# Linear recurrence and soft mixture of experts on one core: the last three groups of tokens regrouped, and the engines' written orders drawn up anew

## The chip, the core and the metric

The kernel runs on one core of a Trainium2 chip. A core has a matrix engine (TensorE), a vector engine (VectorE), an engine for activation functions (ScalarE), an engine for general work (GpSimd), an engine that here only issues transfers (SyncE), 16 DMA engines, an on-chip memory (SBUF) and a small accumulator memory (PSUM) that TensorE writes. Each engine works through its own list of instructions in order; between engines there are semaphores. The metric is device time in microseconds (us); lower is better.

## The reference

The input is x, r_gate and i_gate, each 4 batches x 5056 tokens x 256 channels in float32. Cut to what matters:

```python
log_a = 8 * sigmoid(r_gate) * log(clip(sigmoid(a_param)))      # per channel
a     = exp(log_a)
gated = sqrt(max(1 - a*a, 1e-6)) * sigmoid(i_gate) * x
for t in range(5056):                                          # per batch
    h = a[:, t] * h + gated[:, t];  y[:, t] = h
x = y.reshape(20224, 256)
logits = x @ phi                                               # 256 x 32 slots
d = exp(logits - logits.max(0)); d /= d.sum(0) + 1e-9          # over all tokens
slots = d.T @ x                                                # 32 slot inputs, 4 for each of 8 experts
slot_out[e] = relu(slots[e] @ w1[e]) @ w2[e]                   # w1: 256 x 1024, w2: 1024 x 256
c = exp(logits - logits.max(1)); c /= c.sum(1) + 1e-9          # over the 32 slots
out = c @ slot_out                                             # 20224 x 256
```

The softmax over tokens needs the maximum of each slot over all 20224 tokens. The kernel keeps a running maximum and rescales its running sums when a new group of tokens raises it.

## The kernel before

**Tiles.** The 20224 tokens are 40 quads (q) of 512, the last of 256. Quads are taken in units (p): quad 0 alone, then pairs, then quad 39 alone, 21 units. For logits and sums the quads are put in 11 groups (g): quads 0 to 2, then four quads each up to group 9 (quads 35 to 38), and group 10, which is quad 39 as two pieces of 128.

**Steps of a unit, with their names in the order table.** Loads of r, i and x (Dr, Di, Dx; SyncE). TensorE turns r into the channel layout (TR), ScalarE takes a tanh of it (SR, line 805) and an exponential (EX, 872), which gives the decay a. GpSimd squares it (SQ, 856), ScalarE takes the square root of 1 minus that (RT, 887). The input gate (SI) is, by a letter of the string IV for each unit, a sigmoid (S, line 818), or a tanh (820) that GpSimd turns into a sigmoid with one affine step (P; P1, line 831), or a tanh whose affine step is left to TensorE (E). GpSimd multiplies gate and x (U, 840), TensorE turns the product (TU, 906), VectorE multiplies it by the root (ST, 923) and runs the recurrence as a scan (SC, 940), by halves of 128 channels. TensorE turns the result back (TY, 963), VectorE or ScalarE copies it from PSUM (YC, 979 and 977).

**Steps of a group.** Logits (LG, 1013), running maximum on VectorE (LE, 1026; for the two-piece group 10 two copies fill the column of the maxima, 1025), difference to it (LD, 1047), transposes (TE, 1061), exponential (ES, 1071), sums over the group's tokens on TensorE (AC, 1091), a factor that rescales what was summed before (DM, 1078), the running sum on VectorE (AE, 1107).

**After the last group.** The four rows of maxima are merged (MT, MX, MR, MC, WJ, WE, W; 1275 to 1286), the slot inputs are formed (SP, 1292; SL, 1302; their denominator DN, RD), the first expert layer (L1, 1340) goes to a copy (HS, 1357 on ScalarE or 1359 on VectorE), transposes (HT, 1366) and a relu (HR, 1375) into a tile that was zeroed (HZ, 1320). Then the second layer (L2, 1388), a copy of its result (SO, 1409 and 1411), a scaling (RS, 1416; SH, 1418).

**The combine**, once for each group: logits turned (CT, 1452), exponential (CE, 1469), sums and reciprocals (CM, CS, 1466; RR, 1473 to 1475), normalised weights (CN, 1483), their split in a high and a low part (CH, 1487; CL, 1490), transposes (HP, 1537), a copy (HE, 1548), the product with the expert results (OT, 1567), a copy from PSUM (OE, 1581) and the output transfer (OD, SyncE).

**What sets the order.** The order of each engine is written out in the table ORDER by these names (TY35.2 is the second half of quad 35, AC9.0 the first block of group 9, OT7.4 a part of group 7); a planner only gives buffers to them. Between the entries of TensorE it puts rows of two dummy transposes (line 1220) where it reckons a gap, up to a time WARMT. ScalarE's functions come from tables: tanh and exp lie in one, sigmoid in another, sqrt in a third. Where two entries that follow each other need different ones, a load of the table is put between (ACT_TABLE_LOAD).

## Time and profile before

| | |
|---|---|
| median of 3 runs | 296.96 us (295.51 to 297.18) |
| profiled execution | 296.8 us |
| its span | 295.0 us |
| mean granted TensorE clock | 0.969 of full speed |
| busy in the span: TensorE, VectorE, ScalarE, GpSimd | 248.3, 235.4, 248.8, 204.6 us |
| moved by DMA | 100.05 MB, of it written 20.71 MB |

A row of the timeline gives the start and the duration of an instruction, the engine, its line, its operation, out<-in with partitions x elements, and how many instructions the row holds; in brackets stands how long the engine was idle before it, and what ended that. The table by stretches gives busy time of each engine in a stretch of the span. The chain of waits follows back, from the end, what released each step. Durations of TensorE in one row can hold overlaps with its neighbours.

### The profile page before, as it was taken

The numbers are of one execution on the slowest core, as the hardware profiler recorded it, in microseconds if no ns is written. First come the engines' busy times: TensorE is split into PE (matmuls) and PEld (weight loads), VectorE is DVE, ScalarE is ACT, GpSimd is POOL, SyncE is SP. The second block draws the span as 40 slices with busy tenths as digits, with TensorE's granted clock in tenths as the row PEclk, the third lists the DMA queues.
The fourth block names the chain that finished last, engine by engine and source line by source line (L and its number), as shares of the span: only waits on it lengthen the run. The fifth ranks groups of instructions, "written<-read, shape, count | busy, mean of one in ns | idle before, by whom it ended". The sixth has DMA issues, their size and how long they took to land.

```text
span 295.0 us, 6123 instructions
## 1 busy us (share of the span) xinstructions
PE 248.3 (84%) x2374; PEld 192.0 (65%) x2374; DVE 235.4 (80%) x289; ACT 248.8 (84%) x269; POOL 204.6 (69%) x152
## 2 busy tenths in 40 slices
...
GB/s 236 408 409 410 403 407 412 397 410 368 326 412 195 310 410 410 355 73 247 379 411 363 281 371 127 335 391 392 398 407 290 2 123 420 407 397 415 395 420 242
DMA packets 27553, 100.05 MB, mean 339 GB/s; under 512 B 3074, under 2 KB 3076, under 8 KB 25220
## 3 DMA queue, kind: packets, MB, share of 16 engines
...
q14 instruction: 10, 0.08, 0.1%
...
HBM read 78.94 MB, written 20.71 MB: 338 GB/s over the span
## 4 chain that ended last, share of the span: by engine, by line
ACT 30%; DVE 22%; PE 21%; issue 11%; DMA 5%; POOL 5%; SPq 2%; DVEq 0%; POOLq 0%; ACTq 0%
DVE b L940 9%; DVE pair L923 5%; DMA b<-in_x_dram 5%; ACT b L805 5%; ACT b L872 4%; PE pair L906 4%; ACT b L887 4%; ACT b L818 3%; ACT b L1581 3%; PE bank L1567 3%; ACT L887 2%; PE bank L1388 2%; ACT yn L977 2%; DVE yn L979 2%; PE bank L1537 2%
## 5 line engine op out<-in xcount | busy, mean ns | idle before, releaser
L840 POOL TENSOR_TENSOR b<-b,b 128x1024 f32<-128x1024 f32 x36 | 84.6, 2374 | 4.0 <-ACT b L805 1.6
L856 POOL TENSOR_TENSOR b<-b 128x1024 f32<-128x1024 f32 (+2 forms) x41 | 73.4, 1811 | 12.8 <-ACT b L872 12.7
L923 DVE SCALAR_TENSOR_TENSOR pair<-b,pair 128x1024 f32<-128x1024 f32 (+2 forms) x42 | 48.1, 1157 | 10.0 <-PE pair L906 7.4
L906 PE MATMUL pair<-ident,b 128*128 128x128 f32 x380 | 49.8, 278 | 7.2 <-DVE b L940 3.5
L906 PEld LDWEIGHTS pair<-ident,b 128*128 128x128 f32 x380 | 42.5, 143 | 14.7 <-issue 5.9
L940 DVE TENSOR_TENSOR_SCAN b<-b,pair 128x1024 f32<-128x1024 f32 (+6 forms) x26 | 47.5, 1848 | 0.3
L794 PE MATMUL pair<-ident,st 128*128 128x128 f32 x316 | 42.3, 281 | 6.3 <-DVE b L940 3.1
L940 DVE TENSOR_TENSOR_SCAN b<-b,b,pair 128x1024 f32<-128x1024 f32 (+2 forms) x22 | 45.3, 2073 | 0.3
L794 PEld LDWEIGHTS pair<-ident,st 128*128 128x128 f32 x316 | 35.0, 143 | 13.8 <-DVE b L940 5.2
L872 ACT ACTIVATE b<-b,ca 128x2048 f32<-128x2048 f32 (+3 forms) x24 | 42.4, 1792 | 0.2
L805 ACT ACTIVATE b<-pair 128x1024 f32<-128x1024 f32 (+1 forms) x40 | 39.2, 1014 | 2.6 <-PE pair L794 2.5
L963 PE MATMUL one<-ident,b 128*128 128x128 f32 x196 | 31.0, 288 | 7.0 <-DVE yn L979 5.3
L1483 POOL TENSOR_TENSOR b<-b,rs_all 128x512 f32<-128x512 f32 (+2 forms) x11 | 10.6, 961 | 33.5 <-DVE rs_all L1475 27.3
L963 PEld LDWEIGHTS one<-ident,b 128*128 128x128 f32 x196 | 22.6, 146 | 16.0 <-DVE yn L979 9.3
L887 ACT ACTIVATE b<-b 128x2048 f32<-128x2048 f32 (+2 forms) x17 | 29.5, 1780 | 0.1
L1567 PE MATMUL bank<-bd,hT 64*128 64x256 f32 x252 | 24.4, 295 | 3.1 <-ACT hT L1548 2.4
L1581 ACT COPY b<-bank 128x512 f32<-128x512 f32 x42 | 23.2, 618 | 3.4 <-PE bank L1567 3.4
L818 ACT ACTIVATE b<-b 128x2048 f32<-128x2048 f32 x14 | 26.0, 1902 | 0.1
L979 DVE COPY yn<-one 128x512 f32<-128x512 f32 x33 | 22.2, 685 | 2.9 <-PE one L963 2.6
L1567 PEld LDWEIGHTS bank<-bd,hT 64*128 64x128 f32 x252 | 20.3, 193 | 6.0 <-ACT hT L1548 3.8
L1091 PE MATMUL one<-yn,eS 128*32 128x257 f32 x312 | 20.8, 384 | 1.5 <-DVE yn L979 1.0
L1013 PE MATMUL one<-b,phi_sb 128*32 128x512 f32 x156 | 20.6, 601 | 0.6 <-DVE yn L979 0.6
...
## 6 DMA issues: line engine op xcount, KB each, us to landing
...
```

Source lines behind the costliest of these rows:

```text
L794: nc.tensor.transpose(out=o[:, m, :], in_=raw("r", q)[:, m * D + h * P : m * D + (h + 1) * P], identity=ident,)
L805: nc.scalar.activation(dst, t(rp)[:, :, :c], AF.Sigmoid if SIGR else AF.Tanh, scale=1.0 if SIGR else 0.5)
L818: nc.scalar.activation(v, v, AF.Sigmoid)
L840: eng.tensor_tensor(out=o, in0=a, in1=b, op=ALU.mult)
L856: eng.tensor_tensor(out=t(Nb[p])[:, h, :c], in0=v, in1=v, op=ALU.mult)
L872: nc.scalar.activation(v, v, AF.Exp, scale=ca[:, h : h + 1], bias=ca[:, h : h + 1])
L887: nc.scalar.activation(v, v, AF.Sqrt, bias=quarter if f != 1.0 else f, scale=-f)
L906: nc.tensor.matmul(o[:, m, :], raw(nm, q)[:, m * D + h * P : m * D + (h + 1) * P], ident, is_transpose=True, start=(nm == nms[0] and m == ...
L923: nc.vector.scalar_tensor_tensor(v, t(Nb[p])[:, h, :c], 0.5e-3 if gate_of(quads(p)[0]) == "E" else 1e-3, v, op0=ALU.max, op1=ALU.mult)
L940: nc.vector.tensor_tensor_scan(dst, dst, flat()[:, s0:s1], init, op0=ALU.mult, op1=ALU.add)
L963: nc.tensor.transpose(out=flat()[:, b * D + h * P : b * D + (h + 1) * P], in_=tokens(q, b0 + b, 1)(h), identity=ident,)
L1567: nc.tensor.matmul(t(ops[x])[:, k * D : (k + 1) * D], t(hT)[r, c], T["bd"][0][r, part, :], start=(part == 0), stop=(part == 1),)
```

## The change

The table ORDER is written anew for all five lists. Beside it:

- IV gives the last three units P in place of S, S and P: the gates of units 18 and 19 become a tanh and an affine step for each quad (P135 to P138). P1 may now also stand on VectorE, and P10, P11, P12 and the square SQ0.0 of the first units do.
- Groups 9 and 10, the last 2304 tokens (MERGE): both maxima go to one column of M, the maximum of group 10 starting from that of group 9. The differences of both (LD9, LD10) are taken to the joint maximum; there is one factor and one running sum, and the sums of both go to one PSUM bank. The two copies that filled the column of group 10 are gone.
- DM is now the exponential of a difference of two columns that GpSimd takes first (DD).
- The last three quads are turned back and copied by halves of 128 channels (BYH, mk_yh) in place of halves of the tokens: YC37.0 holds the first half of the channels of quad 37, and needs only the first of the two scans.
- HZ is a copy with scale 0 on ScalarE; HS is on ScalarE; SO is one copy of 256 columns on VectorE.
- WARMT is 200 in place of 60. OT, OE and OD are named and cut by unit; there are 22 output transfers as before.
- The parameters LATE1, GROUPING, SI2, RT2 and YP4 are new and have values that change nothing.

The core of the diff (all of ORDER and of the output's regrouping is left out):

```diff
-IV = 'PPEEEESSSSSSSSSSSSSSP'
+IV = 'PPEEEESSSSSSSSSSSSPPP'
-WARMT = 60.0
+WARMT = 200.0
+BYH = 3
+MERGE = True
...
-            g = add("POOL", f"P1{q}", 0.05 + 0.262 * n, deps=[g], prio=q - 2, emit=e_p1, uses=[st[("i", q)]])
+            g = add(("POOL", "DVE"), f"P1{q}", 0.05 + 0.262 * n, deps=[g], prio=q - 2, emit=e_p1, uses=[st[("i", q)]],
+                    alt={"DVE": 0.07 + 0.22 * n})
...
+    def mk_yh(q):
+        for h in range(H):
+            def e_ty(h=h, yp=yp):
+                for b in range(nb):
+                    nc.tensor.transpose(out=t(yp)[:, b * P : (b + 1) * P], in_=tokens(q, b, 1)(h), identity=ident)
...
+    def mcol(g):
+        return NGR - 2 if MERGE and g == NGR - 1 else g
...
-                lS(g)[:rows, :L], t(lp)[:rows, :L], 0.0, NEG if g == 0 else M[:rows, g - 1 : g],
-                op0=ALU.add, op1=ALU.max, accum_out=M[:rows, g : g + 1],
+                lS(g)[:rows, :L], t(lp)[:rows, :L], 0.0, NEG if g == 0 else M[:rows, prev : prev + 1],
+                op0=ALU.add, op1=ALU.max, accum_out=M[:rows, mg : mg + 1],
...
+        joint = MERGE and g >= NGR - 2
+        le = LE[NGR - 1] if joint else LE[g]
+        acc = shared["acc"] if mg != g else Buf(ONE, f"acc{g}")
...
-                nc.scalar.activation(
-                    dm[:rows, g : g + 1], M[:rows, g : g + 1], AF.Exp, bias=M[:rows, g - 1 : g], scale=-1.0
-                )
+                nc.gpsimd.tensor_tensor(out=dm[:rows, g : g + 1], in0=M[:rows, g - 1 : g], in1=M[:rows, g : g + 1], op=ALU.subtract)
+                nc.scalar.activation(dm[:rows, g : g + 1], dm[:rows, g : g + 1], AF.Exp)
...
+        if joint and mg == g:
+            return
...
-    t_hz = add("POOL", "HZ", 1.6, deps=[ST[(NP - 1, H - 1)]], prio=500, alloc=[hz],
-               emit=lambda: nc.gpsimd.memset(t(hz), 0.0))
+    t_hz = add("ACT", "HZ", 1.95, deps=[ST[(NP - 1, H - 1)]], prio=500, alloc=[hz],
+               emit=lambda: nc.scalar.activation(
+                   t(hz).rearrange("p a b -> p (a b)"), ident[:, 0:1].broadcast_to([P, 4 * QT]), AF.Copy, scale=0.0))
...
-        a = add(("ACT", "DVE"), f"HS{k}", ...
+        a = add("ACT", f"HS{k}", ...
...
-    t_so = add("DVE", "SO", 0.2, deps=[l2_prev], prio=-60, uses=[so], alloc=[soSb], emit=lambda: e_so(0))
-    t_so = [t_so, add("ACT", "SO1", 0.17, deps=[l2_prev], prio=-60, uses=[so, soSb], emit=lambda: e_so(1))]
+    t_so = add("DVE", "SO", 0.38, deps=[l2_prev], prio=-60, uses=[so], alloc=[soSb],
+               emit=lambda: nc.vector.tensor_copy(out=t(soSb), in_=t(so)[:, :D]))
```

The list of VectorE behind the last scans, of the table: before "LE9 LE10 YC38.0 AE8 MX MR YC37.0 YC38.2 WJ W AE9 AE10 SL RR1", now "LE9 LE10 AE8 LD10 YC37.1 MX YC38.1 MR WJ YC39.1 W YC39.0 RR0 AE10 RR1 SL".

ScalarE in the last units, before, from the load of the sigmoid's table for units 18 and 19 to the load behind the root of unit 18 (818 is the gate, 805 the tanh of r, 977 a copy turned back, 887 the root, 1078 the factor):

```order
L818 ACT_TABLE_LOAD
L818 ACTIVATE b_74<-b_74 128x2048
L805 ACTIVATE b_67<-pair_92 128x2x256
L818 ACTIVATE b_70<-b_70 128x2048
L977 COPY yn_81<-one_87 128x2x256
L887 ACT_TABLE_LOAD
L887 ACTIVATE b_70<-b_70 128x2048
L977 COPY yn_76<-pair_92 128x2x256
L1078 ACT_TABLE_LOAD
L1078 ACTIVATE dm<-M 128x1
```

and now, the same place (850 is the gate, 908 the exponential of a, 1163 the factor, 1153 the exponential of a group, 927 the root, 1020 a copy):

```order
L908 ACTIVATE b_73<-b_73,ca 128x256
L1020 COPY yn_81<-pair_93 128x2x256
L1163 ACTIVATE dm<-dm 128x1
L850 ACTIVATE b_69<-b_69 128x2048
L1153 ACTIVATE eS_85<-one_87 128x512
L927 ACT_TABLE_LOAD
L927 ACTIVATE b_69<-b_69 128x2048
L1020 COPY yn_81<-pair_92 128x2x256
L1020 COPY yn_81<-one_87 128x2x256
L1020 COPY yn_76<-one_86 128x2x256
```

The gate of unit 19 stands among exponentials, without a load of its own, and that of unit 18 does so further ahead; an exponential of the last unit stands ahead of them, and copies follow each other behind the root of unit 18.

GpSimd around the products of units 18 and 19, before (840 is the product with x, 856 a square, 1047 a difference of a group):

```order
L840 TENSOR_TENSOR b_66<-b_74,b_66 128x1024 x2
L1047 TENSOR_SCALAR lD_82<-b_75,M 128x512
L856 TENSOR_TENSOR b_66<-b_69 128x1024
L840 TENSOR_TENSOR b_73<-b_70,b_73 128x1024
L856 TENSOR_TENSOR b_72<-b_67 128x256
L840 TENSOR_TENSOR b_73<-b_70,b_73 128x1024
```

and now (876 is the product, 892 the square, 866 the affine step, 1160 the difference of two maxima, 1129 that of a group):

```order
L892 TENSOR_TENSOR b_69<-b_68 128x1024
L876 TENSOR_TENSOR b_70<-b_66,b_70 128x1024
L866 TENSOR_SCALAR b_69<-b_69,half_sb 128x1024 x2
L892 TENSOR_TENSOR b_74<-b_68 128x1024
L876 TENSOR_TENSOR b_70<-b_69,b_70 128x1024 x2
L1160 TENSOR_TENSOR dm<-M 128x1
L1129 TENSOR_SCALAR lD_82<-b_72,M 128x512
```

Two affine steps (P137, P138) stand ahead of the last square of unit 19 and its two products, and the small square of the last unit has gone behind them; the product U37 is the last but for U39.

TensorE between the sums of the last group and the first expert layer, before (1091 is a sum, 1292 the slot inputs, 1305 their denominator, 1340 the first layer):

```order
L1091 MATMUL one_86<-yn_81,eS_85 32x257
L1091 MATMUL bank_2109<-yn_79,eS_84 32x257 x2
L1292 MATMUL bank_2106<-W,accS 128x32 x2
L1305 MATMUL bank_2106<-accS,W 128x1
L1340 MATMUL one_87<-b_72,yn_77 32x256 x8
L1340 MATMUL one_87<-b_75,yn_77 32x256 x8
```

and now (1175 the sums, 1540 logits turned for the combine, 1386, 1399 and 1435 as 1292, 1305 and 1340):

```order
L1175 MATMUL bank_2146<-yn_76,eS_84 32x257
L1175 MATMUL bank_2146<-yn_77,eS_85 32x257 x2
L1540 MATMUL bank_2143<-ident,b_73 128x4x32 x4
L1540 MATMUL one_86<-ident,b_74 128x4x32 x4
L1386 MATMUL bank_2147<-W,accS 128x32 x2
L1399 MATMUL bank_2147<-accS,W 128x1
L1435 MATMUL bank_2142<-b_67,yn_78 32x256 x8
```

The sums of both groups now go to one bank, and the turned logits of groups 4 and 3 (CT4, CT3) stand between the sums and the slot inputs.

## Rows read from the trace of the kernel before

**Rows 1.** Table by stretches: stretch, length, busy us (count) by engine, PEclk, DMA share, GB/s.

```profile
12.00:156.00 144.00, 124.15 (x1086) 98.14 (x1085) 125.64 (x118) 143.20 (x113) 134.19 (x85) 0.99 0.93 357
162.00:199.86 37.86, 33.72 (x308) 24.31 (x310) 37.08 (x35) 36.16 (x36) 32.30 (x18) 0.95 0.83 304
162.00:212.00 50.00, 45.64 (x424) 32.20 (x422) 48.76 (x46) 48.21 (x54) 35.47 (x22) 0.97 0.88 325
241.00:288.00 47.00, 36.12 (x383) 30.06 (x381) 36.20 (x74) 37.22 (x75) 16.87 (x16) 0.95 0.99 407
```

**Rows 2.** Groups of instructions by shape: count | busy us, mean ns | idle before.

```profile
L887 ACT ACTIVATE b<-b 128x2048 f32<-128x2048 f32 x15 | 27.9, 1905 | 0.1
L979 DVE COPY yn<-one 128x512 f32<-128x512 f32 x33 | 22.2, 685 | 2.9 <-PE one L963 2.6
L887 ACT ACT_TABLE_LOAD x10 | 12.8, 1283 | 0.2
L977 ACT COPY yn<-one 128x512 f32<-128x512 f32 x16 | 9.2, 595 | 0.8 <-DVE pair L923 0.8
L1469 ACT ACTIVATE b<-b 128x512 f32<-128x512 f32 x9 | 5.9, 660 | 0.4 <-DVE b L1466 0.4
L1078 ACT ACTIVATE dm<-M 128x1 f32<-128x1 f32 x9 | 2.7, 301 | 0.6 <-DVE b L1026 0.5
L1025 DVE COPY M<-M 32x1 f32<-32x1 f32 x2 | 0.3, 147 | 0.0
```

**Rows 3.** Chain of waits, 209 to 246 us: start, us, what.

```profile
209.95 1.28 ACT L1469
212.29 0.63 PE bank L1013 x8
216.31 1.92 PE one L1091 x32
218.84 0.48 DVE accS L1107
244.61 0.68 PE one L1452 x4
```

**Rows 4.** Timeline of ScalarE, a copy ahead of the last unit's work.

```profile
195.25 0.59 ACT L977 COPY yn<-pair 128x512 f32<-128x512 f32 x1 [1.11 <-PE pair L963]
```

**Rows 5.** Timeline of GpSimd, at the start and at the product U37.

```profile
12.59 1.13 POOL L831 TENSOR_SCALAR st<-st,half_sb 128x1024 f32<-128x1024 f32 x1 [3.21 <-ACT st L820]
17.43 3.20 POOL L831 TENSOR_SCALAR b<-b,half_sb 128x1024 f32<-128x1024 f32 x2
197.47 2.39 POOL L840 TENSOR_TENSOR b<-b,b 128x1024 f32<-128x1024 f32 x1
```

**Rows 6.** Timeline of VectorE, its first product and its last scans.

```profile
16.62 1.90 DVE L840 TENSOR_TENSOR b<-st,b 128x1024 f32<-128x1024 f32 x1 [8.41 <-DMA b<-in_x_dram]
202.75 2.35 DVE L923 SCALAR_TENSOR_TENSOR pair<-b,pair 128x1024 f32<-128x1024 f32 x2
210.72 1.38 DVE L940 TENSOR_TENSOR_SCAN b<-b,b,pair 128x256 f32<-128x256 f32 x2
```

**Rows 7.** Timeline of the serial stretch, all engines.

```profile
213.13 0.34 DVE L1026 TENSOR_SCALAR_CACHE_REDUCE b<-bank,M 64x128 f32<-64x128 f32 x1
219.38 0.63 PE L1292 MATMUL bank<-W,accS 128*128 128x32 f32 x4 [0.77 <-DVE accS L1107]
220.59 3.66 PE L1340 MATMUL one<-b,yn 128*32 128x256 f32 x64 [0.39 <-DVE yn L1302]
225.91 0.41 DVE L1359 COPY hs<-one 128x256 f32<-128x256 f32 x1
226.37 0.51 PE L1366 MATMUL bank<-ident,hs 128*128 128x128 f32 x2 [0.39 <-DVE hs L1359]
236.29 0.29 DVE L1411 COPY hs<-bank 128x128 f32<-128x128 f32 x1 [3.33 <-PE bank L1388]
236.62 0.27 ACT L1409 COPY hs<-bank 128x128 f32<-128x128 f32 x1 [19.30 <-DVE hs L1411]
```

352 lines of the change are left out of this document (197 added, 155 removed).

## The prediction

> **What bounds the kernel now.** First the table by stretches [rows 1]. From 12 to 156 us ScalarE is busy 143.2 of 144. From 162 to 212 VectorE is busy 48.8 of 50 and ScalarE 48.2, GpSimd only 35.5. From 241 to 288 the DMA engines have a share of 0.99 at 407 GB/s: the 20.7 MB of output need 50.9 us at that rate, whatever the engines do. So the end is fixed by when output can begin, and that by the stretch up to 212 and a serial one behind it, in which ScalarE once idles 19.3 us in one piece (the row at 236.62) [rows 7]. Then the chain of waits [rows 3]: a table load at 209.95, the logits of the last group (212.29), the sums of group 9 (216.31), the last running sum (218.84); behind them the slot inputs (219.38) and the first expert layer (220.59) [rows 7]. Into 212 the chain comes along ScalarE, but the last scan on VectorE ended only at 212.10 (210.72 + 1.38) [rows 6]: the two engines arrive together, and only both earlier help. Last the timelines of single engines [rows 4 to 7].
>
> The profiled execution took 296.8 us, its span 295.0; the median of the runs is 296.96. The sum is made against 296.8, which is 0.16 below that median, a tenth of what can be told.
>
> **The change part by part**
>
> *Table switches.* Following both lists of ScalarE with the function of each entry, I count 26 loads before and 23 now, the difference all between 162 us and the last square root. A load is 1.283 us [rows 2], so 3.9 off.
> The row shows the load alone. The Trainium skill (ScalarE: Activation LUTs, What ACT_TABLE_LOAD costs) adds a drain of about 1.38 us to each switch; three switches would then be worth 8.0 instead of 3.9. No drain stands in these rows.
>
> *Copies moved.* Up to its last square root ScalarE has 30 copies of results turned back (YC) in place of 26, at 0.595 [rows 2] or a little less where one follows the other: +2.3. Two exponentials of the combine (CE0, CE1) now stand ahead of that root, 0.66 at most and one of them narrower [rows 2]: +1.1. One small factor (DM) is gone, -0.3 [rows 2]. Net for ScalarE -3.9 + 2.3 + 1.1 - 0.3 = -0.8. VectorE has five copies fewer up to the last logit maximum: 5 x 0.685 = -3.4 [rows 2].
>
> *What the two make of it.* ScalarE also idles 1.8 us in 162 to 212 (50 - 48.2, rows 1), 1.11 of it for one copy's transposes [rows 4]. If all its waits went, the last group would come 0.8 + 1.8 = 2.6 earlier; if the switches come back as waits, 0. VectorE's -3.4 allows either. I take -1.5, the 0.8 and some 40% of the waits: a list without three switches breaks up less, but a list without any wait is not to be had where three engines feed each other.
>
> *GpSimd.* Four more affine steps (P135 to P138) come to it: 1.13 us where nothing else ran, 1.60 each in the pair at 17.43 [rows 5], so 4.5 to 6.4. Of nine one-column differences (DD) one stands ahead of U37; I price it at 0.15 as the one-column copies on VectorE [rows 2]. One small square, SQ20.0, moves behind U37: 256 columns by halves, a quarter of a 2.39 product [rows 5], -0.6. Net up to U37 4.5 + 0.15 - 0.6 = 4.05. From 162 to the end of U37 (197.47 + 2.39 = 199.86) GpSimd is busy 32.3 of 37.86 [rows 1, 5]: 5.6 idle. If all is filled U37 ends at 198.3, if nothing at 203.9. VectorE needs U37, and some 1.1 of transposes, for the product that began at 202.75 [rows 6], in my forecast at 201.25: U37 must end by 200.15, that is 3.8 of the 5.6 must be filled. I cost it at nothing; without that cover it is the slower rival below.
> At 17.43 VectorE still ran a product with both inputs in SBUF (16.62 to 18.52, rows 6), and the pair of affine steps ended at 20.63, which is 18.52 + 2 x 1.06: they seem to have stood until it was over. The Trainium skill (SBUF — State Buffer, Who interferes with whom) says just this of a GpSimd instruction that reads SBUF while VectorE reads two SBUF operands, and that an instruction with one such operand does not disturb it. Late in the kernel VectorE runs products against PSUM and scans; by this rule the four take 1.13 beside the products, and by 1.60 GpSimd would be 1.9 later. It speaks against the slower rival.
>
> *The start.* x of quad 0 is loaded fourth, and one square and three affine steps go to VectorE, which idled 8.41 before 16.62 [rows 6]. The first scans may start some 2 us earlier, but ScalarE is full from 12 on [rows 1] and keeps its list there: 0, between -0.4 and +0.6.
>
> *Fillers.* 78 rows of two dummy transposes in place of 66, at 0.26 a transpose as in the pair at 226.37 [rows 7]: 6 us more of TensorE, which has 20 idle in 12 to 156 alone [rows 1]. 0.
>
> *The merged last groups.* Out go one running sum (0.48, rows 3, of which 0.1 was bare) and two one-column copies of the maximum (0.3, rows 2). In comes that the difference of group 9 waits for the maximum of group 10. From the start of the last logits, L: before, that maximum ended at 213.47 (213.13 + 0.34, rows 7), L + 1.2, and the sums began at L + 4.0 (216.31 - 212.29, rows 3). Now behind L + 1.1 stand the difference on GpSimd (1.13 as an affine step of twice its width at most, more likely 0.8), four transposes (0.68, as at 244.61), the exponential (0.6) and hand-overs: L + 3.5 to L + 4.0. Yet on VectorE a running sum (0.48), the small difference LD10, two half copies (0.41 each, as 225.91 in rows 7) and two steps on the maximum now stand in a row before the maximum can go out, which TensorE sends before the sums: L + 4.3. So +0.35; from -0.2 to +0.8. The running sum: -0.1.
>
> *CT4 and CT3 ahead of the slot inputs.* Four transposes each, 0.68 (the row at 244.61) [rows 3], in a gap of 0.77 in which TensorE waited for VectorE's sum (the row at 219.38) [rows 7]: 1.36 - 0.77 = 0.6 at most; the earlier single sum and the overlap of one four with the next take some back: +0.4.
>
> *Zeros on ScalarE.* About 1.9, as its other 2048-wide activations (L887) [rows 2], in front of two copies and the exponentials of the last two groups. It can run from L on, while VectorE and GpSimd still prepare those: 0. If it starts 1 us later, +0.5.
>
> *Expert copies on ScalarE, results in one piece.* HS0 stood behind other work on VectorE and TensorE waited 0.39 for it (the row at 226.37) [rows 7]; now ScalarE is free, and the transposes stand one w1 product later: -0.4. The results took 0.29 on VectorE from 236.29, then 0.27 on ScalarE, to 236.89; now one copy of 256 columns, 0.41 [rows 7]: -0.2, of which a step now ahead of SH on VectorE takes 0.1 back. Nothing hides these.
>
> Serial stretch: 0.35 - 0.1 + 0.4 - 0.4 - 0.1 = +0.15, between -0.5 and +1.0.
>
> *Output.* The same 22 transfers from other pieces; the DMA is the bound [rows 1]. With CT3 and CT4 done early the queue may fill sooner: -0.2, between +0.3 and -1.0 (20.7 MB at 415 GB/s instead of 407).
>
> Sum: -1.5 + 0.15 - 0.2 = -1.55 from 296.8: **295.2 us**.
>
> **Rivals**
>
> *The switches come back as waits* (no change). Between two square roots ScalarE now does seven copies in a run, each behind transposes that need a bank, while VectorE was busy 48.8 of 50 [rows 1]. For it: the wait in [rows 4] ended on TensorE. Against it: VectorE has 3.4 us less to do. It gives 296.8 + 0 + 0.15 = 297.0.
>
> *GpSimd becomes the last to arrive* (slower). The place is U37 behind P135 to P138, the wait that of the product at 202.75. With none of the 5.6 idle us filled, that product starts at 203.9 + 1.1 = 205.0, 2.25 late: 296.8 + 2.25 + 0.15 = 299.2; at 1.60 a piece 301.1. It turns slower than before where U37 ends after 201.65 (202.75 - 1.1), that is where less than 2.3 of the 5.6 are filled. For it: ScalarE feeds GpSimd, and its two gates now come ahead of the affine steps on the same path. Against it: these gates stand behind fewer switches, so they come sooner.
>
> *Everything fits* (larger gain): all of ScalarE's waits gone, -2.6, and the denser output, -1.0: 296.8 - 3.6 + 0.15 = 293.35.
>
> **How the numbers follow.** Forecast 0.45 (293.8 to 296.3), no change 0.28, GpSimd late 0.15, larger gain 0.12. About 0.5% (1.5 us) is what a measurement can tell from no change: faster is under 295.5, slower over 298.4. Faster: 0.30 of the forecast's 0.45, the larger gain's 0.12, and 0.08 where "no change" ends low or the output is denser: 0.50. Slower: nearly all of the GpSimd case and a little from the serial stretch's upper bound: 0.16. Same: 0.34. The range for 8 in 10 goes from 292.5, below the larger gain for what the output and the start may add, to 298.4, which leaves out most of the GpSimd case.
>
> **What would show it.** Right: 23 table loads; the last logits near 210.8 in place of 212.29; the first product of unit 19 near 201.2 and not waiting for GpSimd; the first expert layer 8.2 to 8.7 us behind the last logits (before 220.59 - 212.29 = 8.3); no wait for HS0's copy; the output at 405 GB/s or more throughout. Wrong: GpSimd without a gap before U37 and VectorE waiting for its product; ScalarE idle 3 us or more in sum after 162; the sums of groups 9 and 10 starting later than 4.8 us behind the last logits; an output stretch with a DMA share under 0.95.

## The result, and the profile after

The median is **292.05 us** (291.53 to 292.86) against 296.24 of the kernel before in the same comparison: ratio 0.9861 [0.9825, 0.9897]. Faster, as forecast, but by 4.2 us in place of 1.6, and 0.45 below the range. Of the distance to the 295.2 of the forecast 0.56 is its base: the sum started from the profiled 296.8, and the median of the kernel before in this comparison is 296.24.

The profiled execution took 292.26 us, its span 290.5, granted clock 0.984 (before: 296.8, 295.0, 0.969). From the two traces, us:

| stretch | before | after | difference | forecast |
|---|---|---|---|---|
| start of the last logits | 212.29 | 209.16 | -3.13 | -1.5 |
| last logits to first expert layer | 8.30 | 8.59 | +0.29 | |
| first expert layer to the product behind SO | 16.34 | 16.21 | -0.13 | |
| these two, the serial stretch | 24.64 | 24.80 | +0.16 | +0.15 |
| that product to the first output transfer issued | 3.34 | 3.25 | -0.09 | |
| first output transfer to the end of the span | 54.73 | 53.29 | -1.44 | -0.2 |
| sum | | | -4.50 | -1.55 |

The table by stretches of the kernel after, as [rows 1], for the window to 156 us, the one up to the last logits, and the output (window and its length; busy time and instructions of PE, PEld, DVE, ACT, POOL; granted clock, DMA share, GB/s):

```profile
12.00:156.00 144.00, 128.80 (x1131) 102.44 (x1129) 127.37 (x121) 142.94 (x113) 131.41 (x87) 1.00 0.93 358
162.00:212.00 50.00, 45.98 (x441) 32.24 (x442) 48.82 (x50) 48.87 (x60) 41.85 (x32) 1.00 0.99 366
240.00:288.00 48.00, 34.10 (x353) 28.08 (x349) 33.43 (x67) 31.81 (x64) 13.46 (x13) 0.93 1.01 415
```

The first row is as before: ScalarE full, and the products of both kernels run together until 180 us (the maxima of groups 6 and 7 start 0.1 and 0.2 earlier). So all of the 3.13 is won between 180 and 209. In the second row VectorE and ScalarE are both full as before, only over a shorter list; GpSimd has gone from 35.5 to 41.85, with the four affine steps. All of its 8.15 idle us lie behind 198.4: up to there it is busy 36.40 of 36.40. In the third the output moves 415 GB/s where it moved 407.

**VectorE, from 161 us to the maximum of group 9** (the last of 512 columns): until 212.02 before, until 208.93 now. Copies there: 8 before, 4 now, -2.44; its waits 1.24 before, 0.62 now, -0.62; the rest -0.03. Of the waits before, the two of unit 18 (a third, 0.46, stood ahead of the last unit's products at 210.05):

```profile
194.51 1.23 DVE L923 SCALAR_TENSOR_TENSOR pair<-b,pair 128x1024 f32<-128x1024 f32 x1 [0.45 <-PE pair L906]
196.07 1.23 DVE L923 SCALAR_TENSOR_TENSOR pair<-b,pair 128x1024 f32<-128x1024 f32 x1 [0.33 <-PE pair L906]
```

The timeline of VectorE after, around the end of the loop (start, length, engine, line, operation, and in brackets the idle time ahead and who ended it):

```profile
191.61 1.23 DVE L963 SCALAR_TENSOR_TENSOR pair<-b,pair 128x1024 f32<-128x1024 f32 x1 [0.62 <-ACT b L927]
199.69 1.22 DVE L963 SCALAR_TENSOR_TENSOR pair<-b,pair 128x1024 f32<-128x1024 f32 x1
208.27 0.74 DVE L980 TENSOR_TENSOR_SCAN b<-b,b,pair 128x256 f32<-128x256 f32 x1
209.90 0.34 DVE L1099 TENSOR_SCALAR_CACHE_REDUCE b<-bank,M 64x128 f32<-64x128 f32 x1 [0.24 <-PE bank L1086]
```

The first row is the 0.62, a wait for the root of unit 18; before, the products of unit 18 waited for transposes instead. The second is the first product of unit 19, in [rows 6] at 202.75, forecast at 201.2; it waits for nobody. The third is the last scan, which ended at 212.10 before and at 209.01 now.

**ScalarE, from the end of the three roots that stand in a row (units 14, 15 and 17) to the start of the root of unit 20:** 47.71 us before, 43.97 now, -3.74. Nine loads are six, -3.86; 18 copies are 21, but +0.61 only; exponentials of the combine +0.97; small factors -0.38; other exponentials +0.36; waits 1.91 before and 0.31 now, -1.6 (the rest +0.16). The timeline of ScalarE after, behind the root of unit 18:

```profile
188.36 1.28 ACT L927 ACT_TABLE_LOAD   x1
189.66 1.92 ACT L927 ACTIVATE b<-b 128x2048 f32<-128x2048 f32 x1
191.47 0.58 ACT L1020 COPY yn<-pair 128x512 f32<-128x512 f32 x1
191.94 1.08 ACT L1020 COPY yn<-one 128x512 f32<-128x512 f32 x2
192.89 0.61 ACT L1020 COPY yn<-pair 128x512 f32<-128x512 f32 x1
193.37 1.11 ACT L1020 COPY yn<-one 128x512 f32<-128x512 f32 x2
194.32 0.65 ACT L1020 COPY yn<-pair 128x512 f32<-128x512 f32 x1
194.80 1.97 ACT L927 ACTIVATE b<-b 128x2048 f32<-128x2048 f32 x1
...
201.52 1.08 ACT L1020 COPY yn<-one 128x512 f32<-128x512 f32 x2 [0.31 <-PE one L1006]
```

One load serves two roots, with seven copies between them that begin 0.48 us apart and wait for nothing: this is the run of copies that the first rival took for the place where the switches come back as waits. The 0.31 is the only wait of the stretch.

**GpSimd** after (the affine steps L866, the products L876, the difference of two maxima L1160):

```profile
176.41 2.26 POOL L866 TENSOR_SCALAR b<-b,half_sb 128x1024 f32<-128x1024 f32 x2
189.66 2.24 POOL L866 TENSOR_SCALAR b<-b,half_sb 128x1024 f32<-128x1024 f32 x2
193.69 4.75 POOL L876 TENSOR_TENSOR b<-b,b 128x1024 f32<-128x1024 f32 x2
198.38 0.22 POOL L1160 TENSOR_TENSOR dm<-M 128x1 f32<-128x1 f32 x1
```

U37 is the second product of the third row and ends at 198.4, which the forecast gave for "all of the idle time filled" (198.3). GpSimd had indeed no gap from 162 us to there. Its transposes run on TensorE from 198.50 to 199.59, and the product of VectorE that needs them starts at 199.69: GpSimd came in time by 0.1 us. The affine steps took 1.13 and 1.12 each.

**The serial stretch** on TensorE after (logits, sums of both groups, two fours of logits turned for the combine, slot inputs, first expert layer), and the first output issue on SyncE:

```profile
209.16 0.63 PE L1086 MATMUL bank<-b,phi_sb 128*32 128x128 f32 x8
213.27 2.37 PE L1175 MATMUL bank<-yn,eS 128*32 128x257 f32 x36
215.57 0.75 PE L1540 MATMUL bank<-ident,b 128*128 128x128 f32 x4
216.16 0.65 PE L1540 MATMUL one<-ident,b 128*128 128x128 f32 x4
216.64 0.53 PE L1386 MATMUL bank<-W,accS 128*128 128x32 f32 x4
217.75 0.85 PE L1435 MATMUL bank<-b,yn 128*32 128x256 f32 x12 [0.39 <-DVE yn L1396]
```

```profile
237.21 0.95 SPq L1678 DMA_DIRECT2D out_dram<-b  x2
```

The sums begin 4.11 behind the last logits (4.0 before [rows 3]; forecast 4.3). The running sum ended at 216.25 and the slot inputs began only at 216.64, behind the two fours: 0.39, where before they began 0.06 behind it (219.32 to 219.38). CT3 and CT4 cost 0.33 there; the forecast had 0.4.

The +0.16 holds for this execution alone. TensorE waited 0.34 in it for the weights of the second layer. The serial stretch is the same in a_copies, a_gates, a_start and a_w100 below, and took 24.33 or 24.34 in each: 0.3 less than before.

**The granted clock.** TensorE's share by 2 us, before, and the same stretches after (columns as above):

```profile
150.00:152.00 2.00, 0.71 (x7) 0.47 (x5) 2.00 (x2) 1.99 (x2) 2.00 (x2) 1.00 1.02 408
152.00:154.00 2.00, 0.03 (x1) 0.03 (x1) 2.00 (x3) 2.00 (x2) 1.89 (x2) 0.99 1.02 406
154.00:156.00 2.00, 2.00 (x10) 2.00 (x11) 1.62 (x4) 1.98 (x2) 2.00 (x2) 0.50 1.04 414
...
190.00:192.00 2.00, 0.62 (x4) 0.42 (x3) 2.00 (x3) 1.99 (x3) 2.00 (x3) 0.88 1.00 396
192.00:194.00 2.00, 2.00 (x12) 2.00 (x11) 2.00 (x2) 1.97 (x4) 2.00 (x2) 0.50 1.02 394
194.00:196.00 2.00, 2.00 (x16) 2.00 (x16) 1.29 (x2) 0.89 (x3) 1.70 (x1) 0.77 1.06 422
```

```profile
190.00:192.00 2.00, 1.52 (x14) 1.18 (x11) 1.38 (x2) 2.00 (x3) 2.00 (x3) 1.00 1.05 350
192.00:194.00 2.00, 2.00 (x18) 1.68 (x16) 1.97 (x2) 2.00 (x6) 2.00 (x2) 1.00 0.91 279
```

Before, TensorE idled and then worked at the lower of its two levels (0.50, that is 1.2 GHz), at 154 to 158 and again at 190 to 196. At the end of the second of these stretches VectorE idled too: 0.45 and 0.33 us ahead of the products at 194.51 and 196.07, for TensorE's transposes, 0.78 of its 1.24. After, the clock is 1.00 in every slice from 100 to 200.

### The profile page after: what moved, and what is told of

The parts are those of the page before. It is cut to its first block, busy times and chain, and to the rows that moved or that the text cites. A ratio compares the mean times of both kernels' runs of the same rounds, so it can differ in the third digit from the quotient of the medians.

```text
span 290.5 us, 6146 instructions
## 1 busy us (share of the span) xinstructions
PE 249.8 (86%) x2398; PEld 192.1 (66%) x2398; DVE 237.0 (82%) x292; ACT 245.2 (84%) x265; POOL 203.8 (70%) x159
## 5 line engine op out<-in xcount | busy, mean ns | idle before, releaser
L876 POOL TENSOR_TENSOR b<-b,b 128x1024 f32<-128x1024 f32 x34 | 80.6, 2394 | 6.8 <-DMA b<-in_x_dram 4.0
L892 POOL TENSOR_TENSOR b<-b 128x1024 f32<-128x1024 f32 (+1 forms) x40 | 73.2, 1847 | 14.4 <-ACT b L908 12.7
L946 PE MATMUL pair<-ident,b 128*128 128x128 f32 x380 | 49.3, 276 | 7.0 <-DVE b L980 4.5
L963 DVE SCALAR_TENSOR_TENSOR pair<-b,pair 128x1024 f32<-128x1024 f32 (+2 forms) x42 | 48.2, 1151 | 7.9 <-ACT b L927 4.6
L1006 PE MATMUL one<-ident,b 128*128 128x128 f32 x192 | 29.0, 279 | 4.7 <-DVE yn L1022 3.4
L1647 PE MATMUL bank<-bd,hT 64*128 64x256 f32 x240 | 26.2, 299 | 3.3 <-ACT hT L1629 1.8
L1006 PEld LDWEIGHTS one<-ident,b 128*128 128x128 f32 x192 | 21.2, 141 | 10.8 <-DVE yn L1022 5.8
L1647 PEld LDWEIGHTS bank<-bd,hT 64*128 64x128 f32 x240 | 21.5, 193 | 6.7 <-ACT hT L1629 2.7
L1578 POOL TENSOR_TENSOR st<-b,st 128x512 f32<-128x512 f32 (+1 forms) x9 | 10.5, 1174 | 17.5 <-DVE st L1575 11.0
L1661 ACT COPY b<-bank 128x512 f32<-128x512 f32 x35 | 19.8, 620 | 3.1 <-PE bank L1647 3.1
L848 ACT ACTIVATE b<-b 128x2048 f32<-128x2048 f32 x12 | 22.2, 1902 | 0.0
L1022 DVE COPY yn<-one 128x512 f32<-128x512 f32 x29 | 19.2, 680 | 0.9 <-PE one L1006 0.9
```

The lines of the kernel that those rows point to most:

```text
L876: eng.tensor_tensor(out=o, in0=a, in1=b, op=ALU.mult)
L892: eng.tensor_tensor(out=t(Nb[p])[:, h, :c], in0=v, in1=v, op=ALU.mult)
L946: nc.tensor.matmul(o[:, m, :], raw(nm, q)[:, m * D + h * P : m * D + (h + 1) * P], ident, is_transpose=True, start=(nm == nms[0] and m == ...
L963: nc.vector.scalar_tensor_tensor(v, t(Nb[p])[:, h, :c], 0.5e-3 if gate_of(quads(p)[0]) == "E" else 1e-3, v, op0=ALU.max, op1=ALU.mult)
L1006: nc.tensor.transpose(out=flat()[:, b * D + h * P : b * D + (h + 1) * P], in_=tokens(q, b0 + b, 1)(h), identity=ident,)
L1647: nc.tensor.matmul(t(ops[x])[:, c * D : (c + 1) * D], t(hT)[r, o : o + (P - 1) * ns + 1 : ns], T["bd"][0][r, part, :], start=(part == 0), ...
```

## The experiments

Four theories, named by letters. **V**: VectorE was the engine that set the end of the loop; what shows is the copies taken off it, and the gates only make ScalarE's room for them. **S**: the switches alone are the gain. **C**: the copies alone are. **Q**: a piece is worth something only in lists drawn up with it. The clock and the early combine are tried beside them. A run whose name begins with b_ is the kernel before with the edit shown, one with a_ the changed kernel with it; "..." marks entries left out. "L" is the start of the last logits in the profiled execution; where a run stood earlier or later from the first product on, that offset is taken off and "net" says so. Runs of the kernel before differ among themselves by some 4 us (294.2 to 298.5), so a median over many is what a ratio rests on.

### Parts of the change in the kernel before

**b_gates**, the gates alone, three loads fewer:

```diff
-IV = 'PPEEEESSSSSSSSSSSSSSP'
+IV = 'PPEEEESSSSSSSSSSSSPPP'
 ScalarE
-SI35 SR39 SI37 YC31.0 RT18.0 YC32.0 DM7 YC30.2 ES7 EX20.0
+SI35 SR39 EX20.0 SI37 DM7 ES7 YC31.0 RT18.0 YC32.0 YC30.2
 GpSimd
-U35 U36 LD7 SQ19.1 U38 SQ20.0 U37
+LD7 P135 P136 U35 U36 P137 P138 SQ19.1 U38 U37
```

> The kernel before with the input gates of units 18 and 19 as tanh and affine step, and the exponentials of the last unit and of group 7 put ahead of the roots of units 18 and 19, so that three table loads go (ScalarE -3.9 us); no copy changes its engine. Theory V (VectorE has no room between 161 and 212 us, and only what leaves VectorE moves the last logits): VectorE's list is the same, and only part of its 1.2 us of waits can go: 0 to -1 us, some 295.7. Rival S (the table switches on ScalarE are the gain): -2.5 us, some 293.7. In the trace: last logits at 211.5 to 212.3 by V, at 209.8 by S.

On TensorE the transposes TE7 go ahead of TY30.0 with it. 297.59, ratio 1.0057 [1.0034, 1.0080]; L 212.59, 0.3 later. Three loads off ScalarE gave nothing, so S falls.

**b_copies**, four copies from VectorE's list to ScalarE's:

```diff
 VectorE
-SC15.0 YC28.0 ST16.0 YC26.0 SC16.0 ... ST17.1 YC31.2 SC17.1 YC30.0 ST18.1
+SC15.0 ST16.0 SC16.0 ... ST17.1 SC17.1 ST18.1
 ScalarE
-SR38 YC25.2 EX18.0 YC26.2 ... YC31.0 RT18.0 YC32.0 DM7 YC30.2
+SR38 YC28.0 YC25.2 EX18.0 YC26.0 YC26.2 ... YC31.0 YC31.2 RT18.0 YC32.0 DM7 YC30.0 YC30.2
```

> The kernel before with four late copies of turned-back results (YC28.0, YC26.0, YC31.2, YC30.0) on ScalarE in place of VectorE, all table switches as before. VectorE -2.4 us, ScalarE +2.0 us between 161 and 212. Theory V with ScalarE arriving at the same time: ScalarE is now late, the last square root comes up to 2 us later: between 0 and +2 us, some 297. Rival C (the copies alone are the gain): -2.4 us, some 293.8. Last logits at 212.3 to 214 by V, at 209.9 by C.

297.85, ratio 1.0073 [1.0038, 1.0107]; its profiled execution was its longest, so only the ratio is used. C falls. That ScalarE had no room for four copies more (busy 48.2 of 50 in [rows 1]) fits; no trace of this run is used to show it.

**b_both**, both edits:

```diff
 ScalarE
-SI35 SR39 SI37 YC31.0 RT18.0 YC32.0 DM7 YC30.2 ES7 EX20.0
+SI35 SR39 EX20.0 SI37 DM7 ES7 YC31.0 YC31.2 RT18.0 YC30.0 YC32.0 YC30.2
```

> Both edits together on the kernel before: three table loads fewer on ScalarE and four late copies from VectorE to ScalarE; merged groups, serial stretch, output and fillers as before. Theory V: VectorE is relieved and ScalarE has the room: -2.4 to -3.1 us, some 293.5, last logits near 209.5. If fillers or the later stages carried the gain: under 1 us off, over 295.3.

297.02, ratio 1.0052 [1.0029, 1.0074]; L net -0.1, where V expected -2.4 or more, and that although its trace shows no fall of the clock up to 212 us. The expectation failed, and the trace says where. TensorE and ScalarE in it:

```profile
200.08 1.09 PE L906 MATMUL pair<-ident,b 128*128 128x128 f32 x8 [1.62 <-POOL b L840]
```

```profile
201.65 0.59 ACT L977 COPY yn<-one 128x512 f32<-128x512 f32 x1 [2.44 <-PE one L963]
```

TensorE's transposes for U37 waited 1.62 for GpSimd, whose product ended at 200.03; the transposes of a copy stood behind them in TensorE's list, and ScalarE idled 2.44 for that copy. The time is there, given back to an order drawn up for other work.

**b_order**, b_both with that order mended by hand:

```diff
 ScalarE
-RT16.0 YC27.0 ... ES6 YC23.2 SI35
+RT16.0 YC27.0 SI35 ... ES6 YC23.2
 TensorE
-TU19.0 TY32.2 TU19.1
+TY32.2 TU19.0 TU19.1
 GpSimd
-LD6 U32 U31 U33 U34 SQ18.0 SQ19.0 SQ18.1 LD7 P135 P136 U35 U36 P137 P138
+U32 U31 LD6 U34 U33 P135 P136 U35 SQ19.0 LD7 SQ18.0 SQ18.1 U36 P137 P138
```

> The kernel before with the gates and the four copies as in b_both, and beside that three places of the order as in the changed kernel: the gate of unit 18 earlier on ScalarE; on GpSimd the affine steps and products of unit 18 ahead of the squares of units 18 and 19; on TensorE the transposes of quad 32's second half (TY32.2) ahead of those of unit 19's product (TU19.0), which wait for GpSimd. Theory Q (ScalarE's and VectorE's freed time only counts when GpSimd's product U37 comes in time and TensorE's list doesn't stand behind it; in b_both ScalarE waited 2.44 us for TY32.2): last logits 2 to 3 us earlier than before, some 293 where before gives 295.6. Rival: the list isn't it, as b_both: over 296. Counted from the first roots at 18 us, since the span's start differs by up to 1 us from run to run.

299.82, ratio 1.0121 [1.0077, 1.0164]: worse, and not as expected. VectorE, TensorE:

```profile
182.73 0.69 DVE L979 COPY yn<-one 128x512 f32<-128x512 f32 x1 [3.43 <-PE one L963]
```

```profile
179.01 1.92 PE L1013 MATMUL one<-b,phi_sb 128*32 128x512 f32 x16 [3.02 <-ACT yn L977]
```

Group 7's logits waited 3.02 for a PSUM bank that a copy on ScalarE had to empty (the releaser in the second row), and VectorE 3.43 for what stood behind them. A copy that changes its engine also changes when its bank comes free.

**b_warm**, more of the dummy transposes in the kernel before:

```diff
-WARMT = 60.0
+WARMT = 200.0
```

> The kernel before with WARMT 200 in place of 60: ten more rows of two dummy transposes between 60 and 200 us, nothing else. Rival W (the granted TensorE clock, which fell to half at 154 and 191 us in the kernel before and not in the changed one, cost the late stretch its time): the clock stays at full and 1.2 us of VectorE's and some of ScalarE's waits go: -1 to -2 us, some 294.8. Theory V: of VectorE's waits 0.8 ended on transposes: 0 to -0.8, some 295.9.

296.08, ratio 1.0022 [0.9996, 1.0048]. Both clock falls are still there (0.75, 0.50, 0.90 from 154 on; 0.63, 0.51 from 192 on): nothing.

**b_fill**, four dummy transposes where TensorE idles ahead of the second fall:

```diff
         for h in range(H):
+            for _ in range(4 if g == 7 else 0):
+                nc.tensor.transpose(out=t(ep)[:, :P], in_=ident, identity=ident)
```

> The kernel before with four dummy transposes in front of the transposes of group 7 on TensorE, which wait there for GpSimd (1.38 us idle at 190 in the kernel before, ahead of a fall of the granted clock to half until 195). Nothing else. Theory W (the fall costs the last logits about 1.2 us: with the same lists b_ct had no fall there and its last logits came 1.3 us earlier, counted from unit 2): no fall at 190 to 195, last logits 1.2 us earlier; in time 0 to -1.2, some 295. Rival: the fall comes all the same (the idle 1.08 us ahead of it stays) and nothing changes.

In the profiled execution the second fall is gone (1.00 from 186 to 198, where the kernel before has 0.88, 0.50 and 0.77 from 190 to 196):

```profile
192.00:194.00 2.00, 2.00 (x20) 1.91 (x19) 2.00 (x2) 1.98 (x3) 2.00 (x2) 1.00 1.01 389
194.00:196.00 2.00, 2.00 (x20) 1.66 (x22) 2.00 (x3) 1.99 (x6) 2.00 (x2) 1.00 1.05 412
```

VectorE no longer waits there, and the lead grows by 1.2 between 189 and 210. The median is not lower: 296.92, ratio 1.0019 [0.9992, 1.0045].

What one fall costs the trace shows. For the executions without a trace the mean granted clock of each is on record. Of 139 executions of the kernel before in these comparisons, the 24 with 0.980 or more have a median of 295.1 us, the 53 under 0.974 one of 296.95. The twelve of b_fill had 0.972 to 0.979, so these four transposes did not keep the clock up over the executions. The four of the changed kernel had 0.975 to 0.984 and took 291.5 to 292.9, in no order of the clock. Its median is 3.1 below that of the 24, in place of 4.2: about 1 us of the whole gain goes with the clock. That a low mean clock goes with a longer time is shown; which falls make it up in each execution is not.

**b_ct**, CT3, CT4 and their steps moved ahead of the slot inputs in the kernel before:

```diff
-CG = 3
+CG = 8
 TensorE
-AC9.3 AC10.0 SP DN ... HP0.0 HP0.4 CT3 ... OT1.0 OT1.4 CT4
+AC9.3 AC10.0 CT4 CT3 SP DN ... HP0.0 HP0.4 ... OT1.0 OT1.4
```

> The kernel before with the combine of groups 3 and 4 begun in the serial stretch: CT4 and CT3 in the gap ahead of the slot inputs, their maxima, subtraction, exponential and sums between the expert layers, as in the changed kernel; all up to the last logits as before. Theory O (the output stretch was not the DMA's alone: its rate fell to 352 and 320 GB/s in two slices, at 22 and 32 us behind its start, where a unit wasn't ready): the two dips go, -0.7 us, against +0.4 for the two turns ahead of the slot inputs: some 0.3 us faster, 295.3; output rate 414 over the stretch. Rival D (the DMA is the bound throughout): the dips stay and only the +0.4 shows, 296.

295.38, ratio 0.9975 [0.9947, 1.0004]. Its executions fall in two lots by their mean clock: seven at 0.979 or 0.980 took 294.5 to 295.4, five at 0.971 to 0.973 took 296.3 to 298.0. Its serial stretch is 25.03 against 24.64, +0.4, the size of the forecast's term, though only 0.13 of it stands ahead of the first expert layer. The stretch from the first output transfer to the end is 0.8 shorter (53.94). The output by 2 us, before:

```profile
262.00:264.00 2.00, 1.27 (x17) 1.03 (x17) 1.32 (x4) 2.00 (x5) 0.24 (x1) 1.00 0.85 352
...
272.00:274.00 2.00, 1.58 (x20) 1.41 (x20) 1.73 (x5) 0.20 (x1) 0.36 (x1) 1.00 0.77 320
```

and the same slices of b_ct:

```profile
262.00:264.00 2.00, 1.87 (x27) 1.67 (x25) 1.42 (x5) 2.00 (x5) 1.27 (x2) 1.00 1.05 434
...
272.00:274.00 2.00, 1.41 (x20) 1.17 (x20) 1.18 (x2) 1.61 (x4) 0.00 (x0) 1.00 1.03 418
```

The mean share of 0.99 in [rows 1] hid two dips in which the DMA engines had too little to do (shares 0.85 and 0.77: 2 x 0.15 + 2 x 0.23 = 0.76 us). They are gone here (a smaller one stands nearer the start, 0.88 at 242 to 244) and in every run of the changed kernel. This run also had no fall of the clock at 190 with the same lists, and its lead grew by 1.2 between 189 and 210, as in b_fill.

### Parts taken back out of the kernel after

**a_copies**, four copies back on VectorE:

```diff
 ScalarE
-DM5 SR38 YC28.0 ... SR39 EX18.1 YC26.0 ... RT18.0 YC31.0 YC31.2 YC32.0 YC30.0
+DM5 SR38 ... SR39 EX18.1 ... RT18.0 YC31.0 YC32.0
 VectorE
-AE5 SC16.1 ... YC27.2 ST17.1 ... SC17.0 ST18.1 SC18.1
+AE5 SC16.1 YC28.0 ... YC27.2 ST17.1 YC26.0 ... SC17.0 ST18.1 YC31.2 SC18.1 YC30.0
```

> The changed kernel with four late copies (YC28.0, YC26.0, YC31.2, YC30.0) back on VectorE, all else as it is. Theory V: VectorE is the bound between 161 and 212 and pays 0.61 each: last logits 1.8 to 2.5 us later, some 294.2. Rival S (ScalarE is the bound): no later, or up to 2 us earlier, 290 to 292.

294.62, ratio 0.9939 [0.9913, 0.9966], against 0.9861 of the whole change. L +1.9 net, no fall of the clock: of 4 x 0.61 = 2.44 on VectorE, 1.9 shows; the wait for the root of unit 18 is 0.29 in place of 0.62, which hides a part. V holds.

**a_gates**, the gates of units 18 and 19 as sigmoids again, two loads more, GpSimd without the four affine steps:

```diff
-IV = 'PPEEEESSSSSSSSSSSSPPP'
+IV = 'PPEEEESSSSSSSSSSSSSSP'
 GpSimd
-U34 U33 P135 P136 ... SQ18.1 U36 P137 P138
+U34 U33 ... SQ18.1 U36
```

> The changed kernel with sigmoid gates again for units 18 and 19, put where they cost the fewest loads (ahead of the tanh of quad 37, and between the exponential of group 7 and the root of unit 18): two loads more on ScalarE (+2.6 us), and the four affine steps gone from GpSimd (-4.5 us). Theory Q (all three engines arrive together, so ScalarE's room was needed for the copies): last logits 1.5 to 2.6 us later, some 294.5 where the changed kernel would give 292.3. Rival V alone (only VectorE's list counts): no later, 292.3. Rival G (GpSimd's affine steps held the rest up): earlier, 291.

On ScalarE the gate SI35 goes ahead of SR37 and the exponential ES7 ahead of SI37 with it. 295.47, ratio 0.9962 [0.9939, 0.9985]; L +3.2 net, though two loads are 2.57. VectorE in it:

```profile
177.95 0.48 DVE L1196 SCALAR_TENSOR_TENSOR accS<-accS,dm,one 128x257 f32<-128x257 f32 x1 [1.11 <-ACT dm L1163]
...
195.10 1.23 DVE L963 SCALAR_TENSOR_TENSOR pair<-b,pair 128x1024 f32<-128x1024 f32 x1 [2.06 <-ACT b L927]
```

The loads stand directly ahead of two results that VectorE, full, waits for: a factor (1.11) and the root of unit 18 (2.06). Taken out of the new lists, the copies cost 1.9 and the gates 3.2, where the loop had gained 3.1, and either put into the old lists gives nothing: Q, in both directions. That GpSimd is relieved of its four affine steps here and L comes later speaks against GpSimd as what set the end.

**a_w100**, the last five rows of dummy transposes out:

```diff
-WARMT = 200.0
+WARMT = 100.0
```

> The changed kernel with WARMT 100 in place of 200: the last five rows of fillers (between 100 and 188 us) gone, nothing else. Rival W (the clock): TensorE's granted clock falls to half somewhere between 140 and 200 us and the last logits come 0.5 to 1.5 us later: some 293. Theory Q: TensorE has room, the clock may fall for one slice but under 0.5 us is lost: 292.

293.51, ratio 0.9895 [0.9865, 0.9925]. The run is 0.2 ahead of after until 110 us; then

```profile
110.00:112.00 2.00, 1.47 (x12) 1.01 (x16) 2.00 (x3) 1.98 (x4) 2.00 (x2) 1.00 1.02 418
112.00:114.00 2.00, 2.00 (x19) 0.99 (x12) 2.00 (x4) 1.99 (x2) 2.00 (x2) 0.53 0.84 338
114.00:116.00 2.00, 2.00 (x19) 1.38 (x21) 1.15 (x3) 2.00 (x2) 2.00 (x2) 0.61 0.26 70
```

VectorE loses 0.85 in the last slice, every product from 115 us on is 1.0 later than it was against after, and 0.9 of it reaches L. A fall of TensorE's clock costs about 1 us here although TensorE is not the bound. It does not order the six executions: those with a mean clock of 0.980 and 0.984 took 291.95 and 293.78.

**a_start**, SQ0.0 and P10 to P12 from VectorE back to GpSimd:

```diff
 VectorE
-CA SQ0.0 SQ0.1 P10 U0 P11 P12 ST0.1
+CA SQ0.1 U0 ST0.1
 GpSimd
-const SQ1.0 SQ1.1 U1
+const SQ0.0 P10 SQ1.0 SQ1.1 P11 P12 U1
```

> The changed kernel with the square of quad 0 and the three affine steps of the first units back on GpSimd, in the order of before. By the prediction's step (ScalarE is full from 12 us on, the start is worth 0): 292 to 292.7. By the reading of b_lists3w (a wait of ScalarE at the start stays till the end): 1.2 to 1.5 us slower, 293.7.

293.77, ratio 0.9912 [0.9877, 0.9947]. In its profiled execution the first two products are 1.4 earlier than after's, but ScalarE waits 1.13 at 25.89 and from 43 to 110 us they are level: there the start is worth nothing, as forecast. 1.0 comes at 112 to 116 with the same fall of the clock (0.50, 0.66), which all its dummy transposes did not prevent. What decides whether that fall happens is open. The median is 1.7 above after's, and the fall does not explain that: the profiled execution, with the fall, was the fastest of the six (292.96), and two with a mean clock of 0.984 took 293.55 and 293.69. So what the start is worth over the executions stays open.

**a_nomerge**, the last groups not merged:

```diff
-MERGE = True
+MERGE = False
```

> The changed kernel with groups 9 and 10 kept apart (two columns of M with two one-column copies, two factors, two running sums, two banks), the rest as it is. By the prediction's step (merging costs 0.35 - 0.1): 0.2 to 0.3 us faster, first expert layer 8.3 us behind the last logits. Rival (the one running sum and the two copies saved are worth more than the wait): 0.4 to 0.8 us slower, 9.0 or more behind the last logits.

292.46, ratio 0.9866 [0.9831, 0.99]; last logits to first expert layer 8.59, the same as with merging. It costs nothing and gives nothing.

**a_best**, an attempt at a faster one:

```diff
 ScalarE
-YC35.2 HZ YC38.0 YC37.0 ES10 ES9 WE
+YC35.2 HZ YC37.0 YC38.0 ES9 ES10 WE
 TensorE
-MT TY38.0 TY38.1 TE10 TE9 ... AC10.0 CT4 CT3 SP DN
+MT TY38.0 TE9 TY38.1 TE10 ... AC10.0 CT4 SP DN CT3
```

> The changed kernel with four moves between the last logits and the first expert layer: the exponential of group 9 and its transposes ahead of those of group 10, YC37.0 ahead of YC38.0 on ScalarE, the replicated maximum ahead of YC38.1 on VectorE, and CT3 behind the slot inputs. Expected from the trace of the changed kernel: sums 0.3 us and slot inputs 0.3 us earlier, first expert layer 8.0 us behind the last logits in place of 8.6; some 291.7 where the changed kernel gives 292.3. Rival: the sums wait for the copies, not for the exponential: 8.4 or more.

On VectorE MR goes ahead of YC38.1 with it. 292.02, ratio 0.9851 [0.9815, 0.9886]: not to be told from after. The sums still begin 4.10 behind the last logits, since TensorE's own list is full there (no wait from 209.37 to 213.47); the first layer begins at 8.46 instead of 8.59.

### The new lists in the old code

Five runs asked whether the lists alone, put into the kernel before, give the gain. All keep the old factor, the old last groups and the old halves.

**b_lists**: after's lists from about 165 us to the last logits. The edit is long; of VectorE's list:

```diff
-IV = 'PPEEEESSSSSSSSSSSSSSP'
+IV = 'PPEEEESSSSSSSSSSSSPPP'
-AE5 ST15.0 YC25.0 SC15.0 YC28.0 ST16.0 YC26.0 SC16.0 YC28.2 LE7 ST16.1 YC24.2 SC16.1 ST17.0 AE6 SC17.0
+AE5 SC16.1 ST16.0 LE7 YC27.2 ST17.1 SC16.0 SC17.1 ST17.0 AE6 SC17.0
```

> The kernel before with the changed kernel's lists of all four engines between about 165 us and the last logits, and with its gates (the same 157 instructions plus the four affine steps, three table loads fewer, four copies on ScalarE); start, fillers, separate groups 9 and 10, serial stretch and output as before. Theory L (what the smaller edits lacked is that all four lists are drawn up together: no list stands at its head for another): last logits 2 to 3 us earlier than before, counted from unit 2, some 294 where before gives 296.6, ratio 0.99. Rival (the gain before the last logits comes from the start or the fillers): as b_both, no gain.

298.38, ratio 1.0048 [1.0018, 1.0079]. 2.9 net is lost where the old lists go over into the new (165 to 180 us) and 2.0 won back by 212.

**b_lists_ct**, b_ct's edit with it:

```diff
-CG = 3
+CG = 8
```

> The same and the early combine of groups 3 and 4 as in b_ct. If the two gains add: b_lists less 0.7 in the output stretch, plus 0.4 ahead of the slot inputs: some 293.5, ratio 0.988 against the changed kernel's 0.986, and no dip of the DMA's rate behind the start of the output. If the merged groups, zeros, expert copies and fillers carried part of it: 1 us or more above the changed kernel.

298.26, ratio 1.0045 [1.0019, 1.0071], no different.

**b_lists3**: all of after's lists up to the last logits, the loads' too; of VectorE's list:

```diff
-SC16.0 YC28.2 LE7 ST16.1 YC24.2 SC16.1 ST17.0 AE6 SC17.0 YC27.2 ST17.1
+SC16.1 ST16.0 LE7 YC27.2 ST17.1 SC16.0 SC17.1 ST17.0 AE6 SC17.0
```

> The kernel before with the changed kernel's lists up to the last logits as a whole, the loads on SyncE among them, and its gates; fillers up to 60 us as before, groups 9 and 10 apart, serial stretch and output as before. Theory L2 (in b_lists the lists lost 2.9 us where the old front part met them, at 165 to 180, and won 2.0 back behind; drawn up from the start together they give the whole gain): last logits 2 to 3 us earlier, some 294 where before gives 296.6, ratio 0.991. Rival M (the other edits carry it): last logits no more than 1 us earlier, ratio above 0.996.

297.55, ratio 1.0021 [0.9996, 1.0045], with clock falls at 112 to 118 (0.50) and 160 to 166 (0.50).

**b_lists3w**, the dummy transposes of after with it:

```diff
-WARMT = 60.0
+WARMT = 200.0
```

> The same with fillers up to 200 us as in the changed kernel. Theory L2 with the clock: as b_lists3 and up to 1 us better, since no fall of the granted clock is left ahead of the last logits: last logits 3 us earlier, some 293.5, ratio 0.989. Rival (fillers cost as much as they keep): no better than b_lists3.

297.25, ratio 1.0029 [1.0007, 1.0051]. No falls in the profiled execution, L 211.66; the products of unit 1 are 1.3 later than in after, those of unit 2 1.0: ScalarE waits 1.21 for transposes at 26.81.

**b_lists4w**, P10 to P12 on VectorE with it, as after has them:

```diff
-            g = add("POOL", f"P1{q}", ...
+            g = add(("POOL", "DVE"), f"P1{q}", ...
```

> b_lists3w with the three affine steps of the first units on VectorE, as in the changed kernel: in b_lists3w they stayed on GpSimd, units 1 and 2 came 1.5 us later than in the changed kernel and ScalarE waited 1.21 us at 26 us, which never came back. Theory L2 with the start: 1.5 us earlier from unit 2 on, last logits 2 to 2.5 us earlier than before, some 295 where before gives 296.7, ratio 0.994 or under (serial stretch and output as before). Rival: the start's lateness is taken up by later waits, no change against b_lists3w, ratio 1.003.

295.81, ratio 0.9979 [0.9951, 1.0007], the best of the five; its profiled execution, with falls at 112 to 118 and 160 to 166, was its longest. Against b_lists3w, which has the same lists and no fall, the maxima of its groups are 0.1 later at 109 us, 0.9 behind the first fall and 2.3 behind the second. Without falls it gains nothing either: its six executions with a mean clock of 0.983 or more took 294.5 to 295.8, and the 24 of the kernel before at 0.980 or more have a median of 295.1.

The expectation that the lists carry most of the gain was missed. It seems that they need the code that they were drawn up with; which of its pieces (the factor by way of GpSimd, copies by halves of the channels, the banks) is missed most is open.

## Why the forecast was too small

**The step that failed is "What the two make of it"**: a term mis-sized, with the mechanism right. It gave the loop -1.5 (0 to -2.6); measured -3.13. The step was made on ScalarE's net and its waits; what set the end was VectorE's list, with the copies gone from it, and a fall of the clock that the prediction had not seen.

- *VectorE.* The forecast had the copies (-3.4) and said of them that they allow either outcome. They were the larger part of the answer: VectorE was busy 48.8 of 50 [rows 1], so what is taken off it shows almost whole as long as nobody makes it wait. Copies -2.44 (four of the forecast's five stand in this stretch, 0.61 each from start to start; a_copies: 1.9 of it shows), waits -0.62: some 1.2 less with the fall of the clock gone (b_ct, b_fill), 0.62 more for the root of unit 18. The sum should have been made on the fullest engine of that stretch, with ScalarE's room as the condition.
- *ScalarE.* Net -0.8 was forecast. Loads -3.86 were right (23 in all, forecast 23); but the copies were +0.61, not +2.3: three more of them in this stretch, and in a run each begins 0.48 behind the last where single ones were counted at 0.595 [rows 2]. The waits went almost whole (-1.6 of 1.91), which the forecast held impossible where three engines feed each other. The bound of -2.6 was no bound: it came from those two.
- *The clock.* The prediction never looked at the profile's clock row. Part of what was counted as order was TensorE at half its clock at 190 to 196: without that fall the same lists were 1.2 earlier (b_ct, b_fill). So of the 3.13 at most 1.2 is the missing fall, with about 1.9, as in a_copies, for the copies. That it is gone because the new lists leave TensorE fewer gaps fits the rows; it isn't shown by itself.
- *Table switches.* The Trainium skill (ScalarE: Activation LUTs, What ACT_TABLE_LOAD costs) adds a drain to each load, by which three were worth 8.0. The stretch of ScalarE became 3.74 shorter in all, of which 3.86 loads and 1.6 waits, less what was added. No drain stands in the rows, and 8.0 is excluded. A load can still cost more than itself, when it stands ahead of what a full engine waits for (a_gates: 3.2 for two, 1.6 each).
- *GpSimd.* Nothing, as forecast, but by a margin of 0.1 us: it was busy without a gap from 162 to the end of U37 at 198.4, where the forecast needed 3.8 of 5.6 idle us filled. The first half of its sign of being wrong, no gap ahead of U37, was there; the second, VectorE waiting for the product, was not. The affine steps at 1.13 and 1.12 agree with the Trainium skill (SBUF — State Buffer, Who interferes with whom): beside them ran scans and products with an operand in PSUM. The rival was real: in b_both GpSimd's product cost 1.62 on TensorE and 2.44 on ScalarE. The difference DD took 0.19 to 0.22, not 0.15.
- *Start* 0: so in the trace of a_start from 43 us on, but its median, 1.7 above after's, leaves it open. *Fillers* 0: not refuted, not shown; the run without the last five rows had a clock fall worth 0.9, and so had one with them.
- *Serial stretch* +0.16 for +0.15, and that is luck: four other runs of the same stretch have -0.3, and this one has a wait of 0.34 for the weights of the second layer. Merging 0 in place of +0.25 (a_nomerge). CT3 and CT4 +0.33 here, +0.4 in b_ct for a forecast of +0.4. HZ (1.91 us from 208.88 on ScalarE) ended ahead of the copies, right. No wait for HS, right. From the first layer to the product behind SO those four are 0.6 shorter than before, forecast 0.5. SO took 0.42, forecast 0.41.
- *Output* -0.2 was forecast for a stretch of which it said that "the DMA is the bound". From its first packet to the last but 50 of 2821 the output took 49.2 us instead of 50.2, -0.95: 49.2 or 49.3 in all seven traces of the changed output, 50.1 to 50.5 in the eleven with the old one, 49.5 and 49.6 in the two with the early combine alone (b_lists_ct, b_ct). So the early combine, which fills the dips, is 0.6 to 0.7 of it; the rest goes with the other pieces. Another -0.5 stands between there and the end of the span (3.7, now 3.2), which varies from 2.5 to 3.7 between runs and is not put down to the change.

Of the rivals, "everything fits" came nearest: 293.35, still 1.1 above the profiled execution, since its loop was bounded at -2.6. "Switches come back as waits" did not occur in full: the only waits left are 0.31 on ScalarE and 0.62 on VectorE. Of the forecast's signs for a right reading these were met: 23 loads, unit 19 unhindered, 8.59 behind the last logits, no wait for HS. The output ran at 415 GB/s in the mean, with single 2-us slices down to 389 where 405 or more throughout was expected. The two times were passed: 209.16 for 210.8, and 199.69 for 201.2.
